# A Fourier mix and a low-rank mixer on one core: the beginning put in another order

## The chip, the cores and the metric

The kernel runs on one core of a Trainium2 chip. A core has five engines that work side by side, each through its own list of instructions in order: PE (TensorE, matrix products), DVE (VectorE), ACT (ScalarE), POOL (GpSimd) and SP (SyncE, which here only issues transfers). Transfers run on DMA engines; SP has one queue for them and POOL another. Semaphores tie the lists together. The metric is the device time of one execution in microseconds (us). Lower is better.

## The reference

The input x is 8 batches of 3136 rows by 256 columns, in float32. The first part takes a Fourier transform along the rows and one along the columns and keeps the real part. The second part is a mixer with a low-rank product over the rows (U is 3136 x 32, V is 32 x 3136) and a two-layer network over the columns:

```python
def _attn_ref(x):
    X = np.fft.fft(x, axis=1)
    X = np.fft.fft(X, axis=2)
    return X.real.astype(np.float32)

def _moe_ref(x, U, V, w_ch1, w_ch2):
    xt = x.transpose(0, 2, 1)
    h = xt @ U @ V
    u = x + h.transpose(0, 2, 1)
    ch = np.maximum(u @ w_ch1, 0.0) @ w_ch2
    return (u + ch).astype(np.float32)
```

## The kernel before

**Tables.** The transform over the rows is a matrix product with a table of sines (`tabs[0]`, called tabs in the profile) and one of cosines (`tabs[1]`, called tabc). Both are made on the chip at the start. DVE makes a phase (`phase`, L157 and L159: a multiply-add and a mask), ACT takes its sine (`sine`, L164). Four of the eight row groups are "odd" (`pho`) and are computed in full; four are "even" (`phe`), computed in half and mirrored by a copy on ACT (`mirror_even`, L238). The odd cosines are copies of odd sines, read backwards (`cosine_odd`, L243, on ACT). The even cosines take two steps on ACT (`cosine`, L170 and L171) and a mirror copy. `halve` (L226, DVE) halves one row group of a table.

**U.** U is loaded in two directions (UF by a gather on POOL, UR on SP), folded on DVE (`fold_u`, L181 to L186) and multiplied by the tables on PE (`transform_u`, L214, 32 small products at a time). For the sines this is `us`, for the cosines `uc`; each has four steps: product, copy back into the table by ACT (L219, L220), product, copy back.

**Folding x.** One batch of x at a time lies in `xf` (rows forwards, gathered by POOL: `load_f`) and `xr` (rows backwards, by SP: `load_r`), each in two halves a = 0, 1 on 98 partitions. Row 0 needs its own transfer to the 99th partition (`load_0`, by SP). DVE folds both along the columns (`along_d`, L249 and L251, into EOF_ and EOR_; POOL copies two lone columns, `alone`, L255), then folds the two directions together (`mirror`, L258, into EOS) and the two halves (`half`, L262, into G). G of batch 0 is made in two parts: columns 0 to 127 and 256, 257 first, then columns 128 to 255.

**Transform and mixer.** `seq` (L297) multiplies G by the tables on PE, 8 steps for a batch; ACT copies one product out (L301) and DVE adds and subtracts (L310 to L315). `chan` (L322, L324) is the transform over the columns with two small matrices MSN and MC, made from phases `pd`; ACT writes S and T (L326). `lowrank` (L334, L337) makes the left factor `TA`; its last line (L338, DVE) fills a row of the right factor `VA`. Then the rows of all batches are worked through in 49 chunks of 512: `front` (L360 on PE, L368 on DVE) makes u, `first_product` (L380 on PE, L382 on ACT) the hidden layer, `second_product` (L396 on PE, L402 to L405 on DVE) the output.

**Order.** The beginning, up to `front(0)`, stands in an order written by hand (`manual_schedule`). After it a scheduler orders the instructions of each engine from the order of the calls; the steps of batch b+1 are spread over the chunks of batch b by due times.

Of the kernel before, what the change touches and what calls it, by code (L numbers as in the profile page):

```python
# [27 lines left out]
def kernel(  # L28
# [42 lines left out]
    def load_0(t, dst_f, dst_r, b, w):  # L71


        lo = t.offset + b * S * w
        nc.sync.dma_start(out=dst_f[PQ:KP],
                          in_=bass.AP(t.tensor, lo + (NI - 1) * w,
                                      [[w, 1], [HALF * w, 2], [-w, NI], [1, w]]))
        nc.sync.dma_start(out=dst_r[PQ:KP].rearrange("p a i d -> p a (i d)"),
                          in_=bass.AP(t.tensor, lo, [[w, 1], [HALF * w, 2], [1, NI * w]]))

    def load_x(b):
        for a in range(2):
# [22 lines left out]
    for a in range(2):  # L105
        gather(UF[:PQ, a].rearrange("p i d -> p (i d)"), moe_U, S // 8 - 1,
               xidx[:PQ, 0, a:a + 1], 8 * R, R)
    load_0(x, xf, xr, 0, D)
    for a in range(2):
        load_r(0, a)  # L110
    for a in range(2):
        load_f(0, a)
    lrow = cpool.tile([P, 2, P], FP32, name="lrow")
    pcol = cpool.tile([P, 1], FP32, name="pcol")
    nc.gpsimd.iota(lrow[:], pattern=[[0, 2], [1, P]], base=0, channel_multiplier=0,
# [39 lines left out]
    def phase(y, a_ap, col_ap, bits):  # L155

        nc.vector.tensor_scalar(y.bitcast(FP32), a_ap, col_ap, float(2 ** (23 - bits)),  # L157
                                op0=AL.mult, op1=AL.add)
        nc.vector.tensor_single_scalar(y, y, 2 ** bits - 1, op=AL.bitwise_and)  # L159

    def sine(out_, y, bits, sgn):
        unit = TWO_PI / 2 ** bits
        pp = out_.shape[0]
        nc.scalar.activation(out_, y, AF.Sin, scale=-sgn * unit,  # L164
                             bias=(c_pi if sgn > 0 else c_npi)[:pp])
# [36 lines left out]
    def transform_u(typ):  # L202

        for pk in (1, 0):
            def contract(pk=pk):
                pu = PU[typ, pk] = psum.tile([P, NI, R], FP32, tag="dft", name="pu", bufs=3)
                for io in range(NI):
                    pn = (io + 1) % 2
                    m = kp(io)
                    j0 = NQ - 1 - (4 * 97 + (io + 1) // 2)  # L210
                    ks = ktiles(pk)
                    for n, i in enumerate(ks):
                        w = tabs[typ][:kp(i), i, pn, j0:j0 + 4 * (m - 1) + 1:4]
                        nc.tensor.matmul(pu[:m, io, :], w, GU[pn][:kp(i), typ, i, :],  # L214
                                         start=(n == 0), stop=(n == len(ks) - 1))
# [24 lines left out]

    def cosine_odd(i):

        nc.scalar.activation(cells(1, i, 1, 1, NQ - 1, 0), cells(0, i, NQ - 2, -1, NQ - 1, 1),  # L243
                             AF.Copy, scale=1.0 if i % 4 == 0 else -1.0)

    def along_d(a, src, dst, part):
        lo, hi = src[:, a, :, 1:128], src[:, a, :, 255:128:-1]
# [80 lines left out]
    def lowrank(b):  # L328
        d = ST[b]
        pt = psum.tile([R, 256], FP32, tag="dft", name="ptt", bufs=3)  # L330
        n = 0
        for typ in range(2):
            for par in range(2):
                nc.tensor.matmul(pt[:], d["tab"][:, typ, par, :], MDT[typ][:],  # L334
                                 start=(n == 0), stop=(n == 3))
                n += 1
        nc.scalar.copy(TA[b % 2][:R, :], pt[:])  # L337
        nc.vector.tensor_tensor(VA[b % 2][R:R + 1, HALF + 1:S], d["S"][0:1, HALF - 1:0:-1],  # L338
                                d["T"][0:1, HALF - 1:0:-1], op=AL.subtract)

# [74 lines left out]
    def transform(b):  # L415

        yield from fold(b)
        for par, typ in ([(0, 0), (1, 0), (0, 1), (1, 1)] if b == 0 else
                         [(0, 1), (0, 0), (1, 1), (1, 0)]):
            for pn in range(2):  # L420
                yield lambda par=par, typ=typ, pn=pn: seq(b, par, typ, pn)
        for ch in range(4):
            for h in range(2):
                yield lambda ch=ch, h=h: chan(b, ch, h)
        yield lambda: lowrank(b)

    CK = {}
    ST = {}
# [13 lines left out]
    def cosine_even(m, i):  # L442
        cosine(tabs[1][:, i, :, NH - 1:NQ], phe[:, m], 15)
        mirror_even(1, i)
# [12 lines left out]
    alone(0, xr, EOR_)  # L457
    for par in range(2):
        nc.gpsimd.memset(G[1][par][:, :, 258:GW].bitcast(I32), 0)
    for s in range(2):  # L460
        nc.gpsimd.memset(VA[s][:].bitcast(I32), 0)
        nc.gpsimd.memset(TA[s][:], 0.0)
        nc.gpsimd.memset(TA[s][R:R + 1, 0:1], 1.0)
        nc.gpsimd.memset(TA[s][R:R + 1, P:P + 1], -1.0)
    nc.gpsimd.iota(pint[:], pattern=[[0, 1]], base=D, channel_multiplier=-1)
    nc.gpsimd.memset(pint[0:1], P)
# [7 lines left out]
    nc.vector.memset(lrow[:, 1, 0:1], 128.0)  # L474
    nc.vector.tensor_single_scalar(pcol[:], pcol[:], 1.0 / D, op=AL.mult)
    pd = gen.tile([P, 2 * P], I32, name="pd", bufs=1)
    phase(pd[:], lrow.rearrange("p a l -> p (a l)"), pcol[:], 17)
    sine(MSN[:, 0:128], pd[:, 0:128], 17, -1)
    sine(MSN[:, 128:256], pd[:, 128:256], 17, 1)
    cosine(MC[:], pd[:], 17)  # L480
    msr = MSN[0:1].rearrange("p (l two) -> p l two", two=2)
    MDT = [MSN, MC]
    halve(1)
    uc[2]()
    uc[3]()
# [6 lines left out]
    for par in range(2):  # L492
        half(0, par, slice(0, 128))
        half(0, par, slice(256, 258))
    for a in range(2):
        along_d(a, xf, EOF_, 1)
        mirror(a, slice(128, 256), AL.add)
    for par in range(2):
        half(0, par, slice(128, 256))

    nc.gpsimd.dma_start(out=W1[:, 0, :], in_=moe_w_ch1[0:P, :])
    w1t = gen.tile([P, H], FP32, name="w1t", tag="w1t", bufs=1)
    gather(w1t[:], moe_w_ch1, D, pint[:], H, 0)
    for s in range(2):
        nc.gpsimd.dma_start(out=VA[s][:R, :], in_=moe_V)
    nc.gpsimd.dma_start(out=W2[:], in_=moe_w_ch2.rearrange("(j p) d -> p j d", p=P))
    nc.gpsimd.memset(msr[:, :, 0:1], 1.0)
    nc.gpsimd.memset(msr[:, :, 1:2], -1.0)
    nc.gpsimd.tensor_copy(W1[:, 1, :], w1t[:])

    gate = cpool.tile([1, 2], FP32, name="gate")
    nc.sync.dma_start(out=gate[:], in_=xf[0:1, 1, 0, 0:2])
    load_x(1)
# [57 lines left out]
```

## Time and profile before

| | |
|---|---|
| time, median of 3 runs | 504.72 us (503.43 to 505.47) |
| the profiled execution | 505.07 us, span 503.3 us |
| PE busy | 471.4 us (94%) |
| DVE, ACT, POOL busy | 311.3, 281.3, 52.7 us |
| PE's first seq product | 33.86 us after the span's start |
| PE's first product of a chunk (L380) | 51.47 us |

The span runs from the first to the last instruction; the execution's own time is a little longer. The profile names an instruction by line, engine and operation, with output and inputs (`eor<-xr` is written to eor from xr). What ended an idle time is named behind an arrow. "Busy" of PE is a modelled figure, since matrix products overlap.

### The profile page before, as it was taken

The numbers are of one execution on the slowest core, as the hardware profiler recorded it, in microseconds if no ns is written. First come the engines' busy times: TensorE is split into PE (matmuls) and PEld (weight loads), VectorE is DVE, ScalarE is ACT, GpSimd is POOL, SyncE is SP. The second block draws the span as 40 slices with busy tenths as digits, with TensorE's granted clock in tenths as the row PEclk, the third lists the DMA queues.
The fourth block names the chain that finished last, engine by engine and source line by source line (L and its number), as shares of the span: only waits on it lengthen the run. The fifth ranks groups of instructions, "written<-read, shape, count | busy, mean of one in ns | idle before, by whom it ended". The sixth has DMA issues, their size and how long they took to land.

```text
span 503.3 us, 8125 instructions
## 1 busy us (share of the span) xinstructions
PE 471.4 (94%) x3097; PEld 305.1 (61%) x3152; DVE 311.3 (62%) x693; ACT 281.3 (56%) x537; POOL 52.7 (10%) x79
## 2 busy tenths in 40 slices
PE   0659999999999999999999999999999999999997
PEld 0644556666566666666666666666666666666665
DVE  6984999999989776963574345344343344343343
ACT  6564634755466544665456544655466544755662
POOL 4722112222150200200000000000000000000000
PEclk9999999999999999999999999999999999999999
DMA  6596687889869982334223332333223332333433
GB/s 184 117 227 158 145 229 205 193 234 255 210 186 243 292 205 91 94 96 119 64 63 85 105 83 59 110 80 110 63 64 85 107 83 64 104 85 106 125 85 126
DMA packets 83475, 67.13 MB, mean 133 GB/s; under 512 B 53470, under 2 KB 79908, under 8 KB 80284
## 3 DMA queue, kind: packets, MB, share of 16 engines
q1 hardware_dynamic: 79868, 51.86, 39.8%
q0 software_dynamic: 3568, 14.76, 11.3%
q8 instruction: 24, 0.39, 0.3%
q14 instruction: 15, 0.12, 0.1%
HBM read 29.26 MB, written 25.69 MB: 109 GB/s over the span
## 4 chain that ended last, share of the span: by engine, by line
PE 89%; DVE 4%; ACT 3%; DMA 1%; issue 1%; POOL 0%; DVEq 0%; POOLq 0%; ACTq 0%
PE p L396 34%; PE p L380 31%; PE pt L297 14%; PE ph L360 4%; PE pst L322 2%; PE pst L324 2%; DMA uf<-in_moe_U_dram,xidx 1%; PE ptt L334 1%; PE pu L214 1%; DVE phe L157 1%; ACT tabc L171 1%; DVE eor L251 0%; DVE eof L251 0%; DVE eor L249 0%; DVE eof L249 0%
## 5 line engine op out<-in xcount | busy, mean ns | idle before, releaser
L382 ACT ACTIVATE h<-p 128x512 bf16<-128x512 f32 x392 | 218.2, 597 | 147.6 <-PE p L380 137.6
L396 PE MATMUL p<-w,h 128*128 128x256 bf16 x1568 | 203.7, 273 | 1.7 <-DVE o L405 0.8
L380 PE MATMUL p<-u,w 128*128 128x512 bf16 x735 | 201.7, 379 | 3.3 <-DVE u L368 1.2
L396 PEld LDWEIGHTS <-h 128*128 128x128 bf16 x1568 | 153.1, 98 | 60.1 <-DVE o L405 1.4
L380 PEld LDWEIGHTS <-w 128*128 128x128 bf16 x784 | 75.8, 98 | 64.1 <-issue 3.5
L402 DVE TENSOR_TENSOR o<-p,ut 128x4 f32<-128x4 f32 (+1 forms) x100 | 16.5, 165 | 137.6 <-PE p L396 136.5
L297 PE MATMUL pt<-tabc,g 98*128 98x425 bf16 (+1 forms) x256 | 57.1, 349 | 0.0
L297 PEld LDWEIGHTS <-g 98*128 98x128 bf16 (+1 forms) x384 | 38.1, 99 | 31.0 <-issue 3.0
L405 DVE TENSOR_TENSOR o<-p,ut 128x254 f32<-128x254 f32 (+1 forms) x100 | 40.9, 409 | 0.0
L404 DVE TENSOR_TENSOR o<-p,ut 128x254 f32<-128x254 f32 (+1 forms) x100 | 40.9, 409 | 0.0
L301 ACT COPY ev<-pt 128x425 f32<-128x425 f32 x32 | 16.5, 515 | 38.4 <-PE pt L297 29.8
L368 DVE TENSOR_TENSOR u<-ph,S 128x512 bf16<-128x512 f32 (+15 forms) x64 | 35.1, 558 | 0.9 <-PE ph L360 0.9
L368 DVE TENSOR_TENSOR u<-ph,T 128x512 bf16<-128x512 f32 (+15 forms) x64 | 35.0, 557 | 0.0
L297 PE MATMUL pt<-tabs,g 98*128 98x425 bf16 (+1 forms) x128 | 29.8, 357 | 0.0
L360 PE MATMUL ph<-va,ta 128*128 128x512 bf16 (+14 forms) x122 | 28.0, 327 | 0.8 <-ACT ta L337 0.5
L52 POOL DMA_INDIRECT xf<-in_x_dram,xidx x16 | 21.2, 1328 | 52.3 <-DVE eof L251 17.1
L310 DVE TENSOR_TENSOR B<-pt,ev 128x393 bf16<-128x393 f32 (+1 forms) x16 | 9.4, 585 | 23.9 <-PE pt L297 23.9
L322 PE MATMUL pst<-A,mc 128*128 128x392 bf16 (+1 forms) x64 | 21.2, 331 | 0.7 <-DVE A L310 0.7
L214 PE MATMUL pu<-gu,tabs 98*98 98x32 bf16 (+1 forms) x64 | 6.2, 252 | 16.5 <-DVE gu L185 13.0
L258 DVE TENSOR_TENSOR eos<-eof,eor 99x1024 bf16<-99x1024 bf16 (+2 forms) x34 | 21.3, 663 | 0.2
L324 PE MATMUL pst<-B,msn 128*128 128x392 bf16 (+1 forms) x64 | 21.1, 330 | 0.0
L255 POOL CAST eof<-xf 99x16 bf16<-99x16 f32 x16 | 12.3, 776 | 82.9 <-DVE eos L258 53.6
(86 smaller groups left out, 288.7 us busy)
## 6 DMA issues: line engine op xcount, KB each, us to landing
out_dram<-o SPq DMA_DIRECT2D x48, 512.0 KB
xr<-in_x_dram SPq DMA_DIRECT2D x16, 784.0 KB
ut<-u SPq DMA_TRANSPOSE x49
w<-in_moe_w_ch_dram POOLq DMA_DIRECT2D x1, 512.0 KB, 15.4
out_dram<-o SPq DMA_DIRECT2D x4, 128.0 KB
va<-in_moe_V_dram POOLq DMA_DIRECT2D x2, 196.0 KB, 13.5
xf<-in_x_dram,xidx POOLq DMA_INDIRECT x16, 7.7
w<-in_moe_w_ch_dram POOLq DMA_DIRECT2D x1, 256.0 KB, 7.5
```

Of the source, the lines that this page charges most:

```text
L52: nc.gpsimd.indirect_dma_start(out_, None, bass.AP(t.tensor, t.offset, [[w, rows], [1, w]]), bass.IndirectOffsetOnAxis(idx, 0), element_of ...
L258: nc.vector.tensor_tensor(EOS[:, a, :, cols], EOF_[:, a, :, cols], EOR_[:, a, ::-1][:, :, cols], op=op)
L297: nc.tensor.matmul(pt[:], g[:kp(i), i, col:col + P], tabs[t][:kp(i), i, par, :], start=(n == 0), stop=(n == len(mm) - 1))
L322: nc.tensor.matmul(pt[:, :hi - lo], MC[:, h * P:(h + 1) * P], d["A"][:, lo:hi], start=True, stop=False)
L324: nc.tensor.matmul(pt[:, :hi - lo], MSN[:, h * P:(h + 1) * P], d["B"][:, lo:hi], start=False, stop=True)
L360: nc.tensor.matmul(ph[:, col:col + hi - lo], TA[b % 2][:, s * P:(s + 1) * P], VA[b % 2][:, lo:hi], start=True, stop=True)
L368: nc.vector.tensor_tensor(u[:, s, col:col + hi - lo], ph[:, col:col + hi - lo], src, op=AL.add)
L380: nc.tensor.matmul(p1[:], W1[:, s, j * P:(j + 1) * P], k["u"][:, s, :], start=(s == 0), stop=(s == 1))
L382: nc.scalar.activation(k["h"][:, j, :], p1[:], AF.Relu)
L396: nc.tensor.matmul(p2[:, t % w, :], h[:, j, rs], W2[:, j, :], start=(j == 0), stop=(j == JT - 1))
L404: nc.vector.tensor_tensor(o[:, ts, 1:P], p2[:, :w, 1:P], ut[:, ts, 1:P], op=AL.add)
L405: nc.vector.tensor_tensor(o[:, ts, P + 1:D], p2[:, :w, P + 1:D], ut[:, tT, P - 1:0:-1], op=AL.add)
```

## The change

Nothing is added to or taken from the computation; the order of the beginning changes, one kind of copy moves to another engine, and two steps are cut in two.

- DVE makes all eight phases and ACT all eight sine masks first; U's fold follows.
- `cosine_odd` is done by GpSimd (a multiply by 1 or -1) in place of ACT. In GpSimd's list it stands behind the first `alone`.
- GpSimd's zeros (`VA`, `TA`, the tail of G of odd batches) and the index `pint` move behind the first fold of batch 0. A small copy out of G (`gate`) stands ahead of the zeros.
- `us` comes ahead of `uc` throughout.
- The phases and matrices over the columns (`pd`, MSN, MC) move behind the first part of G.
- V's transfers move from one place to two, each behind its zeros; `load_f(1)` moves ahead of the second of them. SP's small gate transfer waits for `w1t` in place of `xf`; then `load_r(1)` and `load_0(1)` follow.
- `load_0` sends the backward row in two transfers, one for each half, written as 16 pieces, and for batch 0 it stands behind `load_r`.
- The last line of `lowrank` becomes a step of its own, `difference`. For batch 0 it comes behind `front(0)`, for the others it is one more step of the spread (26 in place of 25).

```diff
-        nc.sync.dma_start(out=dst_r[PQ:KP].rearrange("p a i d -> p a (i d)"),
-                          in_=bass.AP(t.tensor, lo, [[w, 1], [HALF * w, 2], [1, NI * w]]))
+        for a in range(2):
+            nc.sync.dma_start(
+                out=dst_r[PQ:KP, a].rearrange("p i d -> p (i d)").rearrange("p (e f) -> p e f", e=16),
+                in_=bass.AP(t.tensor, lo + a * HALF * w,
+                            [[w, 1], [NI * w // 16, 16], [1, NI * w // 16]]))
...
-    load_0(x, xf, xr, 0, D)
     for a in range(2):
         load_r(0, a)
     for a in range(2):
         load_f(0, a)
+    load_0(x, xf, xr, 0, D)
...
-        nc.scalar.activation(cells(1, i, 1, 1, NQ - 1, 0), cells(0, i, NQ - 2, -1, NQ - 1, 1),
-                             AF.Copy, scale=1.0 if i % 4 == 0 else -1.0)
+        nc.gpsimd.tensor_single_scalar(cells(1, i, 1, 1, NQ - 1, 0),
+                                       cells(0, i, NQ - 2, -1, NQ - 1, 1),
+                                       1.0 if i % 4 == 0 else -1.0, op=AL.mult)
...
+    def difference(b):
+        d = ST[b]
         nc.vector.tensor_tensor(VA[b % 2][R:R + 1, HALF + 1:S], d["S"][0:1, HALF - 1:0:-1],
                                 d["T"][0:1, HALF - 1:0:-1], op=AL.subtract)
...
-    fold_u()
-    for i in range(0, NI, 2):
-        cosine_odd(i)
-    us, uc = list(transform_u(0)), list(transform_u(1))
-    us[0]()
-    uc[0]()
...
     for m, i in enumerate((7, 5, 3, 1)):
         phase(phe[:, m], krow[:KP, :, NH - 1:], ncol[:KP, i:i + 1], 15)
         sine(tabs[0][:, i, :, NH - 1:NQ], phe[:, m], 15, 1)
         mirror_even(0, i)
-    us[1]()
-    cosine_even(0, 7)
-    uc[1]()
-    cosine_even(1, 5)
-    cosine_even(2, 3)
+    fold_u()
+    halve(0)
     for part in range(2):
         along_d(0, xr, EOR_, part)
     alone(0, xr, EOR_)
-    for par in range(2):
-        nc.gpsimd.memset(G[1][par][:, :, 258:GW].bitcast(I32), 0)
-    for s in range(2):
-        nc.gpsimd.memset(VA[s][:].bitcast(I32), 0)
-        nc.gpsimd.memset(TA[s][:], 0.0)
...
-    halve(0)
+    for i in range(0, NI, 2):
+        cosine_odd(i)
+    us, uc = list(transform_u(0)), list(transform_u(1))
+    us[0]()
+    cosine_even(0, 7)
+    cosine_even(1, 5)
+    us[1]()
     us[2]()
+    cosine_even(2, 3)
     us[3]()
+    uc[0]()
     cosine_even(3, 1)
+    uc[1]()
     for part in range(2):
         along_d(1, xr, EOR_, part)
     alone(1, xr, EOR_)
+    halve(1)
+    uc[2]()
+    uc[3]()
...
+    gate = cpool.tile([P, 4], FP32, name="gate")
+    nc.gpsimd.tensor_copy(gate[0:1, 2:3], G[0][1][0:1, 0, 128:129])
+    for s in range(2):
+        nc.gpsimd.memset(VA[s][:].bitcast(I32), 0)
+        nc.gpsimd.dma_start(out=VA[s][:R, :], in_=moe_V)
+        nc.gpsimd.memset(TA[s][:], 0.0)
...
+        if s == 0:
+            nc.gpsimd.tensor_copy(W1[:, 1, :], w1t[:])
+            nc.gpsimd.dma_start(out=W2[:], in_=moe_w_ch2.rearrange("(j p) d -> p j d", p=P))
+            load_f(1, 0)
+            load_f(1, 1)
+    for par in range(2):
+        nc.gpsimd.memset(G[1][par][:, :, 258:GW].bitcast(I32), 0)
+    nc.sync.dma_start(out=gate[0:1, 0:2], in_=w1t[0:1, 0:2])
...
-    for step in list(transform(0))[8:]:
+    for step in list(transform(0))[8:-1]:
         step()
     setup.close()
     cp = ctx.enter_context(tc.tile_pool(name="cp", bufs=2))
     front(0)
+    difference(0)
```

More of the change, by code (lines that the diff above doesn't have):

```diff
@@ L425, in transform @@
         yield lambda: lowrank(b)
+        yield lambda: difference(b)
     CK = {}
@@ L434 @@
         sine(tabs[0][:, i, :, :NQ], pho[:, m], 15, 1)
-    fold_u()
-    for i in range(0, NI, 2):
-        cosine_odd(i)
-    us, uc = list(transform_u(0)), list(transform_u(1))
-    us[0]()
-    uc[0]()
-    def cosine_even(m, i):
-        cosine(tabs[1][:, i, :, NH - 1:NQ], phe[:, m], 15)
-        mirror_even(1, i)
     for m, i in enumerate((7, 5, 3, 1)):
@@ L457, with cosine_even @@
     alone(0, xr, EOR_)
-    for par in range(2):
-        nc.gpsimd.memset(G[1][par][:, :, 258:GW].bitcast(I32), 0)
-    for s in range(2):
-        nc.gpsimd.memset(VA[s][:].bitcast(I32), 0)
-        nc.gpsimd.memset(TA[s][:], 0.0)
[L463 to L466, printed above, removed]
-    halve(0)
+    for i in range(0, NI, 2):
+        cosine_odd(i)
+    def cosine_even(m, i):
+        cosine(tabs[1][:, i, :, NH - 1:NQ], phe[:, m], 15)
+        mirror_even(1, i)
+    us, uc = list(transform_u(0)), list(transform_u(1))
[3 more added lines that the diff above has]
+    us[1]()
     us[2]()
+    cosine_even(2, 3)
     us[3]()
+    uc[0]()
     cosine_even(3, 1)
+    uc[1]()
     for part in range(2):
@@ L473 @@
     alone(1, xr, EOR_)
[L474 to L482, printed above, removed]
     halve(1)
@@ L494 @@
         half(0, par, slice(256, 258))
+    nc.vector.memset(lrow[:, 1, 0:1], 128.0)
+    nc.vector.tensor_single_scalar(pcol[:], pcol[:], 1.0 / D, op=AL.mult)
+    pd = gen.tile([P, 2 * P], I32, name="pd", bufs=1)
+    phase(pd[:], lrow.rearrange("p a l -> p (a l)"), pcol[:], 17)
+    sine(MSN[:, 0:128], pd[:, 0:128], 17, -1)
+    sine(MSN[:, 128:256], pd[:, 128:256], 17, 1)
+    cosine(MC[:], pd[:], 17)
+    msr = MSN[0:1].rearrange("p (l two) -> p l two", two=2)
+    MDT = [MSN, MC]
     for a in range(2):
@@ L499 @@
         half(0, par, slice(128, 256))
+    nc.gpsimd.iota(pint[:], pattern=[[0, 1]], base=D, channel_multiplier=-1)
+    nc.gpsimd.memset(pint[0:1], P)
     nc.gpsimd.dma_start(out=W1[:, 0, :], in_=moe_w_ch1[0:P, :])
@@ L503 @@
     gather(w1t[:], moe_w_ch1, D, pint[:], H, 0)
-    for s in range(2):
-        nc.gpsimd.dma_start(out=VA[s][:R, :], in_=moe_V)
-    nc.gpsimd.dma_start(out=W2[:], in_=moe_w_ch2.rearrange("(j p) d -> p j d", p=P))
     nc.gpsimd.memset(msr[:, :, 0:1], 1.0)
     nc.gpsimd.memset(msr[:, :, 1:2], -1.0)
[L509 to L513, printed above, removed]
-    for step in list(transform(0))[8:]:
+    gate = cpool.tile([P, 4], FP32, name="gate")
[4 more added lines that the diff above has]
+        nc.gpsimd.memset(TA[s][:], 0.0)
+        nc.gpsimd.memset(TA[s][R:R + 1, 0:1], 1.0)
+        nc.gpsimd.memset(TA[s][R:R + 1, P:P + 1], -1.0)
+        if s == 0:
[6 more added lines that the diff above has]
+    nc.sync.dma_start(out=gate[0:1, 0:2], in_=w1t[0:1, 0:2])
+    for a in range(2):
+        load_r(1, a)
+    load_0(x, xf, xr, 1, D)
+    for step in list(transform(0))[8:-1]:
         step()
```

## The prediction

> **What bounds the kernel now.** I read the busy time by stages first, then the chain of work that ended last, then the timelines of DVE, ACT and POOL over the first 65 us. Stages (start:end and length, then busy us of PE, its weight loads, DVE, ACT, POOL, then clock, DMA share, GB/s):
>
> ```profile
> 0.00:34.00 34.00, 12.31 (x129) 12.22 (x130) 29.50 (x60) 21.92 (x39) 17.97 (x36) 1.00 0.71 174
> 34.00:64.22 30.22, 26.91 (x137) 13.77 (x136) 21.51 (x35) 14.55 (x31) 7.02 (x9) 1.00 0.71 161
> 64.22:200.00 135.78, 134.61 (x870) 85.50 (x887) 121.68 (x230) 73.83 (x141) 25.00 (x31) 1.00 0.84 214
> 200.00:350.00 150.00, 148.98 (x977) 96.55 (x995) 77.63 (x189) 87.33 (x168) 2.72 (x4) 1.00 0.33 90
> ```
>
> From 64.22 us on PE idles 1.2 us in 136 and 1.0 in 150, and the change leaves its products as they are. So time can only move before 64.22, by when PE's unbroken work begins. The chain there (start, us, what):
>
> ```profile
> 3.66 6.86 DMA uf<-in_moe_U_dram,xidx
> ...
> 13.24 2.82 DVE phe L157
> 16.08 1.96 DVE phe L159
> 18.07 0.63 ACT tabs L164
> ...
> 30.30 0.54 ACT tabc L238
> 30.84 0.04 issue
> 30.89 3.13 PE pu L214 x32
> 34.02 11.20 PE pt L297 x48
> ```
>
> U's landing holds the even phases, they hold ACT, ACT's tables hold PE's last U product, and that the first seq product. The two phases of 2.8 and 2.0 us are not work: the next ones take 0.41 and 0.37. The timelines show what lies beside them (start, us):
>
> ```profile
> 13.16 2.89 DVE L157 TENSOR_SCALAR phe<-krow,ncol 99x394 f32<-99x394 f32 x1
> 16.08 1.95 DVE L159 TENSOR_SCALAR phe<-phe 99x394 int32<-99x394 int32 x1
> 17.95 0.41 DVE L157 TENSOR_SCALAR phe<-krow,ncol 99x394 f32<-99x394 f32 x1
> ```
>
> ```profile
> 13.25 0.98 POOL L459 MEMSET g<- 99x504 int32 x2
> 14.18 1.40 POOL L461 MEMSET va<- 128x1568 int32 x1
> ...
> 20.49 0.98 POOL L255 CAST eor<-xr 99x16 bf16<-99x16 f32 x1 [1.95 <-DMA xr<-in_x_dram]
> ...
> 37.03 1.04 POOL L509 CAST w<-w1t 128x1024 bf16<-128x1024 f32 x1 [5.17 <-DMA w1t<-in_moe_w_ch_dram,pint]
> 44.59 0.25 POOL L255 CAST eof<-xf 99x16 bf16<-99x16 f32 x1 [4.03 <-DMA xf<-in_x_dram,xidx]
> ```
>
> DVE's phases stand while POOL's zeros run one after another. The other way round, POOL's lone-column copy, 0.25 us alone, took 0.98 while a fold ran on DVE.
>
> **The change, part by part.**
>
> *Even phases and masks.* DVE is done with the odd phases at 7.60; four even pairs of 0.75 end at 10.6. ACT is done with the odd sines at 8.6, then four sine and mirror pairs of 1.09 (18.07 to 22.49 before) end at 13.0. The old chain (fold, 4.0 us of stalls, late masks) is gone. Two even cosines of 1.75 end at 16.4. What is late next: ACT's copy-back of `us[1]`. In the changed program it waits for the fourth of POOL's cosine copies, which read the same table, and the other two cosines stand behind it in ACT's list.
>
> *When the copies start.* They stand behind POOL's first `alone`, which needs x's row 0, and that transfer is moved behind `load_r`. Before, `alone` ran at 12.87. Of the landings of the second backward half the trace has twelve between 12.1 and 16.0 and two at 20.3 and 20.4: the two DMA engines that also carried row 0. Bounds for the new landing are thus 12.9 and 20.4. With row 0 behind, the two should run like the twelve, all issued 0.7 us sooner (1.3 us of row-0 issues gone from ahead of them, 2.72 to 4.01, and one U row of 0.6 added); then 0.7 us for the forward row (16 pieces on two engines, 38.85 to 39.55 for batch 1) and one large row of 0.5 between. I take 16.5. U may land some 0.5 to 1 us later, as large rows now start sooner; its products have cover until the copies end.
>
> *How long the copies take.* No row shows GpSimd multiplying. Nearest is its cast of 1024 elements in 1.04 us: 784 elements give 0.80. The lower end is that; the upper is twice the 1.04, 2.1, for a reversed two-byte read and an arithmetic step. I take 0.9, by the cast, so 3.6 us for four. ACT loses 4 x 0.77 = 3.1 us that lay in an idle stretch (6.5 us before 18.07): no gain on the path. The Trainium skill's GPSIMD Engine Reference (Elementwise — side-by-side cycle accounting) puts a tight loop at 1.8 cycles an element; at its 1.2 GHz that is an estimate of 1.2 us a copy, and the sum below would be 1.2 us longer.
>
> *Folds beside copies.* At 16.5 DVE starts its two folds of the first half, 1.125 each, from the same landing as POOL. By the 20.49 row a POOL reader waits for the fold that runs; by the 13.16 row DVE then waits until POOL's run of operations ends. I take two folds first: copies from 18.8 to 22.4. Bounds: no wait at all (copies 16.8 to 20.4) and all four folds first (copies end at 24.7).
>
> *From the copies to PE.* ACT: copy-back 0.42, cosine 1.75, copy-back 0.41, cosine 1.84 (all from the chain) = 4.4: 26.8. PE's last U product 3.0 (30.89 to 33.86): 29.9. DVE: two folds 2.25, halve 0.35, first part of G 5.36 (26.16 to 31.52 before), of which its first half-tile comes 0.75 sooner: 22.4 + 7.2 = 29.6. The first seq product starts at about 29.9 in place of 33.86: a gain of 4.0 us.
>
> *Column matrices.* Phases, 0.8 us, stand ahead of G's second part (5.0): it is ready near 36.2, needed 7.5 us after the first product (33.86 to 41.34), at 37.4. MSN and MC are needed at 42. Cost 0; cover 1.2 us, beyond which each microsecond counts.
>
> *POOL's list behind the gate.* The gate copy waits for G's second part (36.2); behind it stand zeros 1.4, V's issue 0.6, TA's zeros 0.7, W1's cast 1.0 (40.0, needed at 29.9 + 17.6 = 47.5), W2's issue 0.9, then the gathers of batch 1. V, issued at 38, has until 46. W2's data took 2.5 us behind V's before: in by 46, needed at 52.8. The gathers took 3.2 us each: 48.9 and 52.1. SP's gate now waits for `w1t` (issued near 24, landing by 32 where it is less crowded than before); the backward loads then have until 51. DVE wants the first gather at 48.9. Cover nil: 0 taken, up to 2 us lost.
>
> *Chunk 1.* In the changed order DVE has, behind u of chunk 0: `difference` 0.9, four folds of batch 1 (4.5) and only then u of chunk 1 (1.3). Before, two folds stood there. PE has 16 products until it needs it, 3.8 us (52.01 to 55.77), so it stands 2.9 us. Work from there to its wait for o (55.77 to 63.40, 7.6 us) now ends at 14.3 us after u, with o ready at 13.3; before, PE went on at 64.22, 12.2 us after u. Loss 2.1, less 0.2 as L338 no longer stands ahead of u, and something regained in the smaller waits behind: 1.7.
>
> *Later batches.* One more SP issue of 0.6 per batch and `difference` as a step: SP and DVE have room behind PE's 99%. Cost 0; without that cover a wait like the 0.82 us before 64.22 for each of seven batches, so -0.5 to +2.
>
> Sum: -4.0 + 1.7 = -2.3 us on the profiled 505.07, so 502.8. The median is 0.35 below the profiled execution: 502.4, and I give 502.5.
>
> **The rivals.**
>
> A, this sum: own range 500.8 to 504.8 (landing 15.5 to 17.5, copies 0.8 to 1.1).
>
> B, copies and folds do not hinder each other: copies end at 20.4, PE starts at 27.9 by ACT's path (DVE's G by 26.6). -6.0 + 1.7 = -4.3: 500.4. For it: the fold beside the 0.98 us copy was not longer than others (1.22 against 1.21). Against: that copy was tiny.
>
> C, slower by the port: strict turns, one copy, one fold, or all four folds first. Copies end 2.3 us later: 504.8, no gain. The Trainium skill's SBUF — State Buffer (two separate sides) says that a DVE operation with two SBUF inputs and a GpSimd one that reads SBUF lock each other out for a whole instruction. The 0.98 us row agrees with that.
>
> D, slower by the copy: GpSimd takes 1.7 to 2.1 us for each. Place: ACT behind `us[1]`. Each 0.1 us costs 0.4; above 0.9 + 2.3/4 = 1.5 us a copy the change loses. At 2.0: +4.4 - 2.3, so 506.8. For it: nothing in this trace shows the operation. Against: zeros, casts and index rows of POOL all run near 0.8 to 1.0 ns an element.
>
> E, slower by the row: row 0's small pieces take turns with the large gathered rows and land at 20.4, +3.9: 506.3. For: the two late engines took 1.0 to 1.2 us for each large row, in turns with the other queue. Against: forward rows came in one stretch for batch 1.
>
> **How the numbers follow.** Chances: A 45%, B 20%, C 12%, D 12%, E 11%. The time is A's. The range leaves out the fast half of B and the slow half of D and E: 499.8 to 506.8. Half a per cent, 2.5 us, is about what a measurement can tell from no change: faster is below 502.2, slower above 507.2. Faster: B and under half of A, 0.40. Slower: the ends of D and E, 0.11. Within: 0.49.
>
> **What would show it.** Right: no zeros beside the phases, phases of 0.4 us; ACT's copy-back of tabs idle some 5 us on POOL's tabc copies; four copies near 0.9 us; first seq product near 30; PE idle about 3 us for u of chunk 1; PE near 99% from 65 on. Wrong: the first `alone` after 18.5 (E), copies over 1.5 us (D), a fold over 1.3 us or not (A against B), DVE waiting for the gather of batch 1, or PE idle over 1% past 70 us.

## The result and the profile after

The changed kernel is slower: 511.31 us (median of 4 runs, 510.82 to 512.11) against 505.10 for the kernel before in the same session, a ratio of 1.0129 (95% interval 1.0100 to 1.0159). The forecast was 502.5, the range 499.8 to 506.8. The profiled execution took 511.09 us with a span of 509.3, 6.0 us longer than before.

Stages of the changed kernel, cut at its own events (start:end and length, then busy us of PE, its weight loads, DVE, ACT, POOL, then clock, DMA share, GB/s):

```profile
0.00:37.10 37.10, 12.63 (x129) 12.27 (x130) 27.89 (x60) 17.48 (x31) 19.98 (x25) 1.00 0.44 120
37.10:54.76 17.66, 15.39 (x71) 7.36 (x72) 7.50 (x18) 7.66 (x19) 10.68 (x21) 1.00 0.94 218
54.76:71.00 16.24, 13.38 (x67) 7.17 (x68) 16.20 (x22) 8.60 (x16) 5.56 (x5) 0.89 0.80 190
71.00:200.00 129.00, 128.20 (x834) 81.88 (x848) 116.01 (x217) 71.31 (x136) 21.82 (x29) 1.00 0.85 220
```

The cuts are the first seq product (37.10, before 33.86), the first product of a chunk (54.76, before 51.47) and 71, by when PE's unbroken work runs again. The first stage is 3.24 us longer, the transform as long as before (17.66 against 17.61). From 54.76 to the end it takes 454.5 us, before 451.8 (503.3 less 51.47). I call this last length the tail: it is 2.7 us longer. From 71 on PE idles 0.8 us in 129, so nothing is lost there. The whole loss of 6.0 lies ahead of 71: 3.3 at the beginning, 2.7 in the tail.

The beginning, in the chain that ended last of the changed kernel (start, us, what):

```profile
4.29 13.70 DMA xr<-in_x_dram
18.11 0.20 POOL eor L259
...
19.34 10.29 POOL tabc L246 x4
...
33.54 0.54 ACT tabc L241
34.13 3.13 PE pu L217 x32
```

x's row 0 is awaited until 18.1, then GpSimd's four copies take 10.3 us, then come ACT's 4.4 and PE's 3.0. The copies are the longest piece that an engine works on. The timelines of the changed kernel show the same by engine (start us, us, engine, line, operation, then idle before and what ended it):

```profile
8.38 0.42 DVE L160 TENSOR_SCALAR phe<-krow,ncol 99x394 f32<-99x394 f32 x1
8.83 0.37 DVE L162 TENSOR_SCALAR phe<-phe 99x394 int32<-99x394 int32 x1
...
20.35 1.84 DVE L253 TENSOR_TENSOR eor<-xr 99x1016 bf16<-99x1016 f32 x1
...
19.34 10.28 POOL L246 TENSOR_SCALAR tabc<-tabs 99x784 bf16<-99x784 bf16 x4
...
29.65 0.34 ACT L222 CAST tabs<-pu 98x224 bf16<-98x224 f32 x1 [13.26 <-POOL tabc L246]
...
22.53 0.27 PE L217 MATMUL pu<-gu,tabc 98*98 98x32 bf16 x1 [3.29 <-POOL tabc L246]
25.40 0.27 PE L217 MATMUL pu<-gu,tabc 98*98 98x32 bf16 x1 [2.60 <-POOL tabc L246]
27.54 0.28 PE L217 MATMUL pu<-gu,tabc 98*98 98x32 bf16 x1 [1.86 <-POOL tabc L246]
29.68 2.85 PE L217 MATMUL pu<-gu,tabc 98*98 98x32 bf16 x29 [1.86 <-POOL tabc L246]
```

The phase stall is gone: phase 0.42, mask 0.37. But ACT stood 13.26 us until the copies were done. PE's U product took them one by one as they came, so its four waits mark their ends: 22.5, 25.4, 27.5, 29.7. The first two ran beside DVE's folds of float32 rows (3.1 and 2.9 us); the third ran beside one fold of EOS (1.30 us, two-byte numbers) and the fourth beside nothing, and both took 2.14.

The tail, in windows of 2 us of the changed kernel (same columns as the stages):

```profile
60.00:62.00 2.00, 0.39 (x1) 0.11 (x2) 2.00 (x3) 0.03 (x1) 1.76 (x1) 1.00 0.17 25
62.00:64.00 2.00, 1.81 (x8) 0.97 (x8) 2.00 (x4) 1.19 (x2) 0.00 (x0) 0.63 0.66 242
64.00:66.00 2.00, 2.00 (x8) 1.04 (x7) 2.00 (x3) 0.07 (x1) 0.00 (x0) 0.51 1.17 291
```

PE stands 2.38 us for u of chunk 1 while DVE is full. Then the granted clock is about 0.5 until 66, and 1.00 behind that. In that time 8 products of L404 take 1.91 us and 4 of L388 1.58; a little later the same take 1.04 and 1.03, so with the first three of L388 (1.14 against 0.81) the lower clock costs about 1.75 us. Stand and clock make 4.1; the 0.82 and 0.31 us that PE stood there before no longer appear, which leaves 3.0 of the measured 2.7.

### The profile page after: what moved, and what is told of

It reads as the page before. It is cut to its first block, busy times and chain, and to the rows that moved or that the text cites. A ratio compares the mean times of both kernels' runs of the same rounds, so it can differ in the third digit from the quotient of the medians.

```text
span 509.3 us, 8153 instructions
## 1 busy us (share of the span) xinstructions
PE 473.2 (93%) x3097; PEld 306.3 (60%) x3152; DVE 309.7 (61%) x693; ACT 279.7 (55%) x533; POOL 59.7 (12%) x84
## 4 chain that ended last, share of the span: by engine, by line
PE 89%; DMA 3%; POOL 2%; issue 2%; DVE 2%; ACT 1%; SPq 1%; DVEq 0%; POOLq 0%
PE p L404 35%; PE p L388 31%; PE pt L301 14%; PE ph L368 4%; DMA xr<-in_x_dram 3%; POOL tabc L246 2%; PE pst L326 2%; PE pst L328 2%; PE ptt L338 1%; PE pu L217 1%; DVE u L376 0%; SPq L75 0%; ACT tabc L174 0%; DVE eof L253 0%; DVE eor L255 0%
## 5 line engine op out<-in xcount | busy, mean ns | idle before, releaser
L388 PE MATMUL p<-u,w 128*128 128x512 bf16 x731 | 202.4, 380 | 4.9 <-DVE u L376 3.7
L404 PE MATMUL p<-w,h 128*128 128x256 bf16 x1568 | 203.7, 273 | 1.7
L404 PEld LDWEIGHTS <-h 128*128 128x128 bf16 x1568 | 153.6, 98 | 59.9 <-issue 0.7
L388 PEld LDWEIGHTS <-w 128*128 128x128 bf16 x784 | 76.0, 98 | 65.1 <-issue 4.2
L301 PEld LDWEIGHTS <-g 98*128 98x128 bf16 (+1 forms) x384 | 38.1, 99 | 32.9 <-issue 3.2
L305 ACT COPY ev<-pt 128x425 f32<-128x425 f32 x32 | 16.5, 515 | 32.9 <-PE pt L301 22.2
L314 DVE TENSOR_TENSOR B<-pt,ev 128x393 bf16<-128x393 f32 (+1 forms) x16 | 9.4, 586 | 27.7 <-PE pt L301 27.5
L52 POOL DMA_INDIRECT xf<-in_x_dram,xidx x16 | 18.8, 1175 | 56.0 <-DVE o L413 22.1
L253 DVE TENSOR_TENSOR eor<-xr 99x1016 bf16<-99x1016 f32 x16 | 20.0, 1251 | 5.7 <-DMA xr<-in_x_dram 5.7
L330 ACT CAST S<-pst 128x392 bf16<-128x392 f32 (+1 forms) x32 | 15.7, 492 | 8.9 <-PE pst L328 8.9
```

The source lines that it names most:

```text
L253: nc.vector.tensor_tensor(dst[:, a, :, 1:128], lo, hi, op=AL.subtract)
L301: nc.tensor.matmul(pt[:], g[:kp(i), i, col:col + P], tabs[t][:kp(i), i, par, :], start=(n == 0), stop=(n == len(mm) - 1))
L388: nc.tensor.matmul(p1[:], W1[:, s, j * P:(j + 1) * P], k["u"][:, s, :], start=(s == 0), stop=(s == 1))
L404: nc.tensor.matmul(p2[:, t % w, :], h[:, j, rs], W2[:, j, :], start=(j == 0), stop=(j == JT - 1))
```

## The experiments

Theory 1: GpSimd is slow at the copies, and they hold ACT and so the first seq product. Theory 2: the late row 0 is the loss. Theory 3: the loss behind the beginning is the order of DVE's work around chunk 1. The rivals of each stand in the expectations. All results, with the first seq product, the first product of a chunk and the tail of the profiled execution (us):

| label | seq | chunk | tail | median | ratio to before (95%) |
|---|---|---|---|---|---|
| before | 33.86 | 51.47 | 451.8 | 504.1 to 505.1 by session | |
| after | 37.10 | 54.76 | 454.5 | 511.31 | 1.0129 (1.0100 to 1.0159) |
| act_copies | 27.96 | 46.40 | 455.6 | 503.97 | 1.0006 (0.9980 to 1.0031) |
| copies_first | 29.45 | 46.72 | 457.1 | 504.16 | 1.0001 (0.9978 to 1.0023) |
| price (one run) | 28.36 | 46.68 | 456.1 | 504.60 | |
| row0_early | 28.91 | 46.66 | 454.5 | 503.87 | 0.9996 (0.9972 to 1.0019) |
| two_copies | 33.30 | 51.68 | 454.5 | 507.98 | 1.0088 (1.0060 to 1.0115) |
| u1_first | 37.74 | 56.29 | 459.8 | 515.01 | 1.0207 (1.0151 to 1.0263) |
| u1_two | 37.30 | 54.27 | 453.4 | 510.35 | 1.0131 (1.0086 to 1.0176) |
| diff_alone | 32.30 | 50.17 | 452.6 | 504.49 | 1.0013 (0.9987 to 1.0039) |
| zeros_late | 29.50 | 47.86 | 451.8 | 501.34 | 0.9936 (0.9913 to 0.9959) |
| late_dve | 29.77 | 47.70 | 451.9 | 501.64 | 0.9949 (0.9928 to 0.9969) |
| best | 25.54 | 43.56 | 455.2 | 501.78 | 0.9951 (0.9928 to 0.9975) |
| early_x | 27.79 | 55.24 | 453.0 | 507.10 | 1.0071 (1.0042 to 1.0100) |

Read the columns with care. The tails repeat: 451.8, 451.8 and 451.9 in before, zeros_late and late_dve, and 454.5 in after, row0_early and two_copies. The starts do not: diff_alone has the beginning of before, yet its seq product came at 32.30, because the first even phase took 0.93 there in place of 2.89. The stretch from the first seq product to the first chunk product does not either. In the same code it took 17.66 us in after, 16.97 in u1_two and 18.55 in u1_first. The first seq products start 0.35 us apart and the later ones 0.18, and it was 14, 10 and 18 products that went at the slower pace. So differences under some 1.6 us between single profiles say little unless they lie in the tail.

**The copies on ACT again (act_copies).**

```diff
-        nc.gpsimd.tensor_single_scalar(cells(1, i, 1, 1, NQ - 1, 0),
-                                       cells(0, i, NQ - 2, -1, NQ - 1, 1),
-                                       1.0 if i % 4 == 0 else -1.0, op=AL.mult)
+        nc.scalar.activation(cells(1, i, 1, 1, NQ - 1, 0), cells(0, i, NQ - 2, -1, NQ - 1, 1),
+                             AF.Copy, scale=1.0 if i % 4 == 0 else -1.0)
```

> Only the engine of the odd cosines is put back: ACT copies them, everything else as in the changed kernel. Theory 1 (GpSimd's copies set the beginning): ACT makes its four copies by 16.2 in its idle stretch, ends its last copy-back near 24.1, PE's last U product ends near 27.1; DVE's folds from 18.07 run unhindered (1.22 each) and the first part of G is ready near 28.1. First seq product near 28.2 in place of 37.1, time near 502.4. Rival (the start is held by something else: row 0's landing at 18.0 or DVE's own work): the first seq product stays later than 33 and the time above 507.

Two lines of PE's timeline in this run:

```profile
27.96 1.60 PE L301 MATMUL pt<-tabs,g 98*128 98x425 bf16 x4 [1.08 <-DVE g L266]
...
54.30 0.39 PE L388 MATMUL p<-u,w 128*128 128x512 bf16 x1 [3.44 <-DVE u L376]
```

The first seq product came at 27.96 as expected, 9.1 us sooner, now held by DVE's G. So, with all else as changed, the copies' engine alone takes the loss at the beginning away; row0_early below shows that this is not the only way. The time is 503.97, level with the kernel before, not 502.4: the tail grew by 1.1 us, because batch 1's x was not there yet (DVE waited 1.07 us for it) and PE stood 3.44 us for u of chunk 1.

**The copies ahead of the first lone-column copy (copies_first).**

```diff
-    alone(0, xr, EOR_)
     for i in range(0, NI, 2):
         cosine_odd(i)
+    alone(0, xr, EOR_)
```

> The copies stay on GpSimd but stand ahead of its first lone-column copy, so that they start when the odd sines are there (8.6) and run beside DVE's phases and U's fold, not beside the folds of x. Theory 1a (GpSimd is slow at this operation by itself): about 2.1 us each, copies end at 17 to 19. Theory 1b (the folds of x stretched them, alone they are as fast as its cast): about 0.9 us each, copies end near 12.5. Either way DVE's path then holds PE: first seq product near 28.2, time near 502.4; if U's fold and the phases are stretched by the copies, up to 2 us more.

Timelines of DVE and POOL in this run:

```profile
7.50 1.49 DVE L160 TENSOR_SCALAR phe<-krow,ncol 99x394 f32<-99x394 f32 x1
9.03 1.31 DVE L162 TENSOR_SCALAR phe<-phe 99x394 int32<-99x394 int32 x1
...
7.93 8.91 POOL L246 TENSOR_SCALAR tabc<-tabs 99x784 bf16<-99x784 bf16 x4
```

Far from the folds of x the four still took 8.91 us, 2.2 each: 1a, not 1b. They stretched DVE in turn: phase 1.49 in place of 0.42, mask 1.31 in place of 0.37, so that PE's first U product came at 17.71 in place of 13.25. DVE lost nothing by it, since it reached x's first fold at 18.25, when x had just landed. PE's U products ended later, so the first seq product came at 29.45, 1.5 us behind that of act_copies. The time is that of act_copies.

**The price of the operation by itself (price).** The copies of the table are on ACT, as above. Three further operations write to a spare tile:

```diff
+    nc.gpsimd.tensor_copy(scr[0:1, 3, 0, 0:1], tabs[0][0:1, 7, 0, 1:2])
+    nc.gpsimd.tensor_single_scalar(scr[:, 0, :, 1:NQ], cells(0, 0, NQ - 2, -1, NQ - 1, 1), -1.0, op=AL.mult)
+    nc.gpsimd.tensor_single_scalar(scr[:, 1, :, 1:NQ], cells(0, 2, 1, 1, NQ - 1, 0), -1.0, op=AL.mult)
+    nc.gpsimd.tensor_copy(scr[:, 2, :, 1:NQ], cells(0, 4, NQ - 2, -1, NQ - 1, 1))
```

> The changed kernel with the odd cosines on ACT, and three more operations on GpSimd into a spare tile, from 14 to 18.4 us, where DVE waits for x and runs nothing: the odd cosine's multiply with its read backwards, the same multiply reading forwards, and a plain copy reading backwards, 784 elements each. Theory 1 (the operation is slow by itself): the first takes 2.0 to 2.3 us with DVE idle. If the backward read is what costs, the second takes about 0.9 and the third about 2.1; if the multiply is what costs, the second about 2.1 and the third about 0.8. Rival (only DVE beside it stretched it): all three 0.8 to 1.1 us.

Timelines of POOL and DVE in this run (L452 multiplies and reads backwards, L453 multiplies and reads forwards, L454 copies and reads backwards):

```profile
14.21 2.19 POOL L452 TENSOR_SCALAR scr<-tabs 99x784 bf16<-99x784 bf16 x1
16.39 2.16 POOL L453 TENSOR_SCALAR scr<-tabs 99x784 bf16<-99x784 bf16 x1
18.50 1.52 POOL L454 COPY scr<-tabs 99x784 bf16<-99x784 bf16 x1
...
18.11 1.22 DVE L253 TENSOR_TENSOR eor<-xr 99x1016 bf16<-99x1016 f32 x1 [4.13 <-DMA xr<-in_x_dram]
19.24 1.85 DVE L255 TENSOR_TENSOR eor<-xr 99x1016 bf16<-99x1016 f32 x1
```

With DVE idle one copy of the table's kind (a multiply, read backwards) takes 2.19 us, and reading forwards changes nothing. The plain copy took 1.52 beside two folds, one of which took 1.85 in place of 1.22. So the operation is slow by itself, and its direction is not the cause; the multiply costs at least 0.6 more than the copy. This is one run.

**Row 0 first again (row0_early).**

```diff
+    load_0(x, xf, xr, 0, D)
     for a in range(2):
         load_r(0, a)
     for a in range(2):
         load_f(0, a)
-    load_0(x, xf, xr, 0, D)
```

> Only batch 0's row 0 is loaded ahead of the backward halves again, as in the kernel before. Theory 2 (the late landing is a part of the loss by itself): the first lone-column copy runs near 13 in place of 18.1, the four copies end 4 to 6 us sooner, near 24, first seq product 31 to 33, time 505 to 507. Rival (the large rows of x land late whatever row 0 does): lone-column copy still after 17, time 510 to 512. By theory 1 the four copies still take 8.4 us or more here.

POOL's timeline in this run:

```profile
11.14 0.25 POOL L259 CAST eor<-xr 99x16 bf16<-99x16 f32 x1 [3.04 <-DMA xr<-in_x_dram]
11.33 10.11 POOL L246 TENSOR_SCALAR tabc<-tabs 99x784 bf16<-99x784 bf16 x4
```

The lone-column copy ran at 11.14 in place of 18.11; the four copies took as long as before, 10.11, but ended 8.2 us sooner. The first seq product came at 28.91 (31 to 33 expected), and the time, 503.87, is below the 505 to 507 expected. So theories 1 and 2 are not rivals: the loss needs a slow copy and a late start, and any one of three edits (act_copies, copies_first, this) brings the time from 1.3% above the kernel before to level with it.

**Two of the four copies (two_copies).**

```diff
+        if i < 4:
+            nc.gpsimd.tensor_single_scalar(cells(1, i, 1, 1, NQ - 1, 0),
+                                           cells(0, i, NQ - 2, -1, NQ - 1, 1),
+                                           1.0 if i % 4 == 0 else -1.0, op=AL.mult)
+            return
+        nc.scalar.activation(cells(1, i, 1, 1, NQ - 1, 0), cells(0, i, NQ - 2, -1, NQ - 1, 1),
+                             AF.Copy, scale=1.0 if i % 4 == 0 else -1.0)
```

> The changed kernel with two of the four odd cosines on GpSimd, the other two on ACT in its idle stretch. By the copies' measured length (the four ended at 22.5, 25.4, 27.5 and 29.7 by PE's waits) ACT's wait ends at 25.4 in place of 29.65, the first seq product comes at 32.9 in place of 37.1, 1.0 before that of the kernel before. Behind it the changed order costs 2.7 us (span less first product of a chunk: 454.5 against 451.8). Time 506 to 507.5: slower than before with an earlier start. Rival (with two copies less the folds of x collide less and the start falls under 31): time 503 to 505.

The two took 6.01 us, the seq product came at 33.30 (32.9 expected), and the time, 507.98, is 0.5 above the 506 to 507.5 expected. The tail is 454.5, as after. The beginning is then no later than before (first chunk product 51.68 against 51.47), and the kernel still loses 0.9%: what remains, 2.7 us in the tails, is the changed order around chunk 1.

**u of chunk 1 at once (u1_first), and behind two folds (u1_two).** The first edit:

```diff
-    front(0)
+    front(0); front(1)
     difference(0)
...
-            if j == 3 and c + 1 < NCH:
+            if j == 3 and 0 < c < NCH - 1:
```

> The changed kernel with u of chunk 1 made right behind u of chunk 0, ahead of the difference and the folds of batch 1; the beginning stays as it is (first seq product at 37.1). Theory 3 (the loss behind the beginning is PE's stand for u of chunk 1 and the lower clock after it): PE does not stand over 0.5 us between 56 and 62, the granted clock stays at 1.00 from 62 to 66 where it was 0.50, time 507 to 508.5. Rival (the loss comes from later batches, 26 steps in place of 25, or PE only stands later for its outputs): time within 1 us of 511.3.

The second:

```diff
-            if j == 3 and c + 1 < NCH:
+            if j == (0 if c == 0 else 3) and c + 1 < NCH:
```

> The changed kernel with two folds of batch 1 ahead of u of chunk 1, as before, in place of four; the difference stays ahead of them, the beginning as it is (first seq product 37.1). Theory 3a (the bunch of folds ahead of one u is the loss): PE stands 0.5 to 1.0 us for u of chunk 1 in place of 2.4 and 0.8 to 1.8 for the outputs or u of chunk 2, the granted clock stays at 1.00; time 508 to 509.5. Theory 3b (DVE has too much work from 54 to 75, whatever its order): PE's stand moves to chunk 2 and is as long, over 2 us, with the clock at 0.50 after it; time 510.5 to 513.

PE's timeline in u1_first:

```profile
71.75 1.89 PE L388 MATMUL p<-u,w 128*128 128x512 bf16 x4 [3.93 <-DVE u L376]
```

And in u1_two:

```profile
68.14 0.72 PE L404 MATMUL p<-w,h 128*128 128x256 bf16 x5 [1.38 <-DVE o L413]
...
69.95 0.60 PE L388 MATMUL p<-u,w 128*128 128x512 bf16 x2 [1.09 <-DVE u L376]
```

With u of chunk 1 at once, its stand was gone and the clock stayed at 1.00 up to 71, but eight folds then stood ahead of u of chunk 2: PE stood 3.93 us there, and the kernel is 0.8% slower than the changed one. My theory 3 as first put fell: the stand moved. With two folds ahead of u of chunk 1 and six ahead of the first outputs, PE's stands are 1.4 and 1.1 us, the clock stays at 1.00 and the tail of the profiled execution is 453.4, 1.1 shorter. The median, 510.35, lies between what 3a and 3b gave, and by the ratios (1.0131 and 1.0129) no gain can be told. By the tails, which are of one profile each, the order of the folds accounts for 1.1 of the 2.7 us and the difference behind u of chunk 0 for 0.8 (the next run). The other 0.8 is not settled by any run.

**The difference as its own step, alone (diff_alone).** To the kernel before:

```diff
+    def difference(b):
+
+        d = ST[b]
...
+        yield lambda: difference(b)
...
-    for step in list(transform(0))[8:]:
+    for step in list(transform(0))[8:-1]:
...
     front(0)
+    difference(0)
```

> The kernel before with one part alone: the difference is a step of its own, behind u of chunk 0 for batch 0 and one of 26 steps for the others. On DVE it then stands ahead of the two folds and of u of chunk 1. Theory (every us that DVE does between u of chunk 0 and the folds of batch 1 is paid): folds start 0.9 us later after u of chunk 0, PE stands about 0.7 us for u of chunk 1 and about 1.7 in place of 0.8 for the outputs; time 0.5 to 1.5 us above the kernel before. Rival (26 steps disturb the later batches): PE idles over 1 us past 100 us, time 2 us or more above.

The tail is 452.6, 0.8 longer than before, with PE's stand for the outputs at 1.4 in place of 0.8 us and a new one of 0.2 for u of chunk 1; the time (ratio 1.0013) can't be told from before. The seq product at 32.30 is no effect of this edit, which leaves the beginning as it is. 26 steps in place of 25 cost nothing that shows: past 70 us PE had no wait.

**The zeros alone (zeros_late).** To the kernel before; W1's issue and `pint` stay ahead of them:

```diff
-    for par in range(2):
-        nc.gpsimd.memset(G[1][par][:, :, 258:GW].bitcast(I32), 0)
-    for s in range(2):
-        nc.gpsimd.memset(VA[s][:].bitcast(I32), 0)
...
     gather(w1t[:], moe_w_ch1, D, pint[:], H, 0)
+    gz = cpool.tile([1, 2], FP32, name="gz")
+    nc.gpsimd.tensor_copy(gz[0:1, 0:1], G[0][1][0:1, 0, 0:1])
+    for par in range(2):
+        nc.gpsimd.memset(G[1][par][:, :, 258:GW].bitcast(I32), 0)
+    for s in range(2):
+        nc.gpsimd.memset(VA[s][:].bitcast(I32), 0)
...
```

> The kernel before with one part of the change alone: GpSimd's zeros wait for the first part of G. Theory (the phase stall held the beginning): the first even phase and mask take 0.4 us each in place of 2.89 and 1.95, ACT's even masks and PE's last U product come 4.0 us sooner, first seq product near 29.9 in place of 33.86, if DVE's G (31.5 before, 4 us sooner too) is ready. The time follows only as far as DVE has room for batch 1's folds: by the runs with an early start so far (starts of 28 to 29, times no lower than before) 0 to 2 us less, 502 to 504; if the whole gain were kept, 500. Rival (something else holds the masks): start at 33 or later, time 504 to 505.

DVE and PE in this run:

```profile
12.85 0.41 DVE L157 TENSOR_SCALAR phe<-krow,ncol 99x394 f32<-99x394 f32 x1
13.30 0.37 DVE L159 TENSOR_SCALAR phe<-phe 99x394 int32<-99x394 int32 x1
...
29.50 1.58 PE L297 MATMUL pt<-tabs,g 98*128 98x425 bf16 x4
```

The phases take 0.41 and 0.37, the seq product comes at 29.50, 4.36 sooner than in the profile of before (2.80 sooner than in diff_alone, where the stall was shorter), the tail is that of before (451.8), and the time is 501.34, 3.6 us below the kernel before in that session (504.93). With one part of the change and none of the rest it beats both kernels, and no other run has a lower median.

**Two edits for the beginning and one for chunk 1 (best).** To the changed kernel: row 0 first (as in row0_early), two folds ahead of u of chunk 1 (as in u1_two), and the copies on DVE:

```diff
-        nc.gpsimd.tensor_single_scalar(cells(1, i, 1, 1, NQ - 1, 0),
+        nc.vector.tensor_single_scalar(cells(1, i, 1, 1, NQ - 1, 0),
...
     halve(0)
+    for i in range(0, NI, 2):
+        cosine_odd(i)
     for part in range(2):
         along_d(0, xr, EOR_, part)
     alone(0, xr, EOR_)
-    for i in range(0, NI, 2):
-        cosine_odd(i)
```

> The changed kernel with three edits: the odd cosines copied by DVE right behind U's fold (0.42 us each, by the halving of 786 elements), row 0 of batch 0 loaded first again, and two folds ahead of u of chunk 1. DVE folds the first backward half from 16, the second from 18.2, G's first part is ready near 26.0; ACT never waits for the copies, PE's last U product ends near 24. First seq product 26.0, first product of a chunk 43.7 in place of 51.47. Behind it 0.5 to 2 us more than in the kernel before: time 498 to 500. Rival (DVE's folds of batch 1 hold PE whatever the start): PE stands over 2 us between 47 and 56, clock 0.50 after it, time 501 to 504.

DVE in this run:

```profile
13.50 1.17 DVE L246 TENSOR_SCALAR tabc<-tabs 99x784 bf16<-99x784 bf16 x4
...
46.63 1.22 DVE L253 TENSOR_TENSOR eof<-xf 99x1016 bf16<-99x1016 f32 x1 [1.53 <-DMA xf<-in_x_dram,xidx]
```

The seq product came at 25.54, 8.3 us sooner than before, and the four copies took DVE 1.17 us together. But the time, 501.78, is no better than zeros_late: the tail is 3.4 longer. DVE waited 1.53 us for batch 1's x and PE stood 1.50, 1.41 and 1.09 us in place of 0.82 and 0.31. The 498 to 500 expected was missed. The time lies in the rival's range, but the rival's signs, a stand over 2 us and a clock of 0.50, do not show.

**Batch 1's x earlier (early_x).** To best: V's zeros and issue ahead of the gathers, the gathers ahead of W1's cast and W2, SP's gate on xf in place of w1t, two folds ahead of u of chunk 0:

```diff
-    nc.gpsimd.tensor_copy(gate[0:1, 2:3], G[0][1][0:1, 0, 128:129])
...
-            nc.gpsimd.tensor_copy(W1[:, 1, :], w1t[:])
-            nc.gpsimd.dma_start(out=W2[:], in_=moe_w_ch2.rearrange("(j p) d -> p j d", p=P))
             load_f(1, 0)
             load_f(1, 1)
+            nc.gpsimd.tensor_copy(W1[:, 1, :], w1t[:])
+            nc.gpsimd.dma_start(out=W2[:], in_=moe_w_ch2.rearrange("(j p) d -> p j d", p=P))
...
-    nc.sync.dma_start(out=gate[0:1, 0:2], in_=w1t[0:1, 0:2])
+    nc.sync.dma_start(out=gate[0:1, 0:2], in_=xf[0:1, 1, 0, 0:2])
...
+    steps = list(transform(1)); steps[0]()
     front(0)
```

> The best kernel so far by its start (DVE copies, row 0 first, two folds ahead of u of chunk 1), with batch 1's x fetched earlier: V's and TA's zeros of even batches stand ahead of GpSimd's wait, the forward gathers directly behind it, W1's cast and W2 behind those; SP's gate waits for batch 0's last forward rows, as in the kernel before; two folds of batch 1 stand ahead of u of chunk 0 on DVE. Theory (the end is set by when DVE can begin batch 1's folds: span less that moment was 451.4 before, 452.2 in the run named best): x lands near 39 to 40 in place of 46.6, two folds are made in DVE's 4.3 us of idle time ahead of u of chunk 0, no wait for the gather; PE stands under 1 us for u of chunk 1; span 494 to 496, time 496.5 to 499. Rival (the landings crowd each other, x lands no sooner than 43 and holds u of chunk 0, or V comes late): time 501 or more.

DVE in this run:

```profile
52.23 1.22 DVE L253 TENSOR_TENSOR eof<-xf 99x1016 bf16<-99x1016 f32 x1 [11.94 <-DMA xf<-in_x_dram]
```

And SP in this run:

```profile
41.38 0.64 SPq L524 DMA_DIRECT2D gate<-xf  x1
...
43.83 0.63 SPq L75 DMA_DIRECT2D xf<-in_x_dram  x1
```

The time is in the rival's range, but the cause is another one, and it lies in the edit. The gathers did come earlier: the first was issued at 30.7 and landed at 37.4 (37.3 and 46.6 in best), and the second had landed by 41.4 (50.6 in best). But SP's gate reads xf and stands behind these gathers, which write to xf. So it waited for batch 1's own rows, until 41.4; the expectation has it wait for batch 0's. Row 0 of batch 1 stands behind the gate on SP: it was issued at 43.83 in place of 30.10 and landed at 52. DVE's two folds waited 11.94 us for it, with u of chunk 0 behind them, and PE stood 10.89 us. So what an earlier x is worth was not tested. The profiled execution is a long one of this kernel (510.0 against a median of 507.1).

**Zeros late, copies on DVE (late_dve).** To zeros_late: `cosine_odd` on DVE behind the even phases, and `uc[0]` behind it.

> The kernel before with two edits: zeros behind the first part of G (as in the run named zeros_late) and the odd cosines copied by DVE behind the even phases, in 1.2 us for four. ACT's 3.1 us of copies are gone, so PE's last U product ends near 26.4; DVE's first part of G, 27.05 in zeros_late, comes 1.2 later, near 28.3. First seq product 28.3 in place of 29.5; x of batch 1 lands at 46.6 as in both faster runs and does not hold DVE. Span 498.0 to 499.0, time 499.5 to 501. Rival (start and x's landing both no sooner): as zeros_late, 501.3.

The seq product came at 29.77, not 28.3, and the time is 501.64, as zeros_late. The rival held: ACT's copies had lain in its idle time ahead of the even phases (it idled 5.39 us there in this run), so taking them away moved nothing. ACT's work still began when U had landed and DVE had made the even phases.

## Why the prediction was wrong

By its own steps:

- *Even phases and masks*: right. Phases 0.42 and 0.37, two even cosines done at 16.4. zeros_late shows what the stall alone was worth: 4.36 us at the first seq product against the profile of before (0.3 of it because U landed sooner), and 3.6 us in the medians.
- *When the copies start*: off by 0.5, by two errors that nearly cancelled. The row landed 1.6 us late, at 18.1 in place of 16.5, but the copies waited for one fold of DVE and not for two, so they started at 19.34 in place of 18.8.
- *How long the copies take*: here the prediction failed. 0.9 us each was taken, by GpSimd's cast of 1024 elements in 1.04, with 2.1 as the upper end. One copy takes 2.19 us alone, above the upper end, and the four took 10.28 in place of 3.6: 6.7 us. The sentence from the Trainium skill's GPSIMD Engine Reference (Elementwise — side-by-side cycle accounting) gave an estimate of 1.2 us for a copy; the run that prices it shows 2.19, nearly twice that, and the measurement decides.
- *Folds beside copies*: the size was small, but the turns were another. DVE did not wait until the copies were done: it went on with its folds beside them. The first two copies lost 1.7 us together to DVE's folds, and one fold took 1.84 in place of 1.22. DVE also waited 3.30 us for a lone-column copy that stood behind the copies on POOL; this was not foreseen, and ACT's path was longer anyway.
- *From the copies to PE*: right, 4.43 and 2.97 us for 4.4 and 3.0.
- *Column matrices* and *POOL's list behind the gate*: right at 0 in the changed kernel. With an earlier start (act_copies, copies_first, best) the wait for batch 1's x that the step named did come, 1.1 to 1.7 us.
- *Chunk 1*: the stand for u of chunk 1 was foreseen, the size of the loss off by 1.0: 2.7 in place of 1.7. PE stood 2.38 us, less than the 2.9 taken, but the granted clock fell to 0.5 behind it, about 1.75 us that no step held.
- *Later batches*: right at 0.

The repaired sum: 502.5 plus 7.2 for the end of the copies (29.6 in place of 22.4) plus 1.0 for the tail is 510.7; 511.3 was measured. Rival D named mechanism, place and break-even point (1.5 us a copy), and was given 12%: its 506.8 was worked out at 2.0 us a copy, without the collisions. Rival E was a part of it, though its own sign did not show (the first `alone` ran at 18.11, and the sign was after 18.5): the late row put the copies on the path, and in row0_early, with it early, copies just as slow cost nothing.

## What to carry to other kernels

When the trace has no row for the operation that an engine takes over, work out first at which price the change turns, and give more chance to the wrong side of it the further the nearest row is in operation and type. Then ask whether the new work stands behind a wait that it does not need: here GpSimd was idle for 10 us ahead of the copies, and moving one line (copies_first) took 7.65 us off the start. A gain at a beginning is kept only as far as what comes next is ready sooner too. zeros_late lost nothing in the tail; of its 4.36 us, 0.75 went between the seq product and the first chunk product, where 18 products in place of 14 went at the slower pace. best, 4 us earlier still, kept none of that. Batch 1's x landed at 46.6 in both, and that this is the reason is argued, not shown, since early_x did not test it.

## What the runs showed of the hardware

- GpSimd took 2.19 us to multiply 99 x 784 two-byte elements by a constant, ACT 0.84 for the same copy in two_copies, and DVE 1.17 for four of them in best.
- A GpSimd operation of this kind slows DVE's short operations beside it: phase 0.42 to 1.49 and mask 0.37 to 1.31 in copies_first, a fold 1.22 to 1.84 in after. The zeros did the same to a phase (2.89) and a mask (1.95) in the kernel before, but beside the folds of zeros_late, where they ran from 28.2 to 32.8, the folds kept their 1.21.
- The granted clock fell to 0.5 for some 3 us or more after PE had stood about 2.4 us or longer (after, row0_early, two_copies, act_copies, copies_first, u1_first, early_x), and stayed at 1.00 after stands of 1.4 to 1.5 us (u1_two, best). The Trainium skill's TensorE: Matmul & The Clock Gate (Part 1: The HAM clock gate) puts the idle window that lowers the clock at about 3.4 us; the trace shows the fall after a stand of 2.38 us, or 3.0 us with one product in it. In early_x it fell at 46.1, under 2 us after the last product that the trace shows. The measurement decides.
- The first 10 to 18 seq products start 0.35 us apart and the later ones 0.18, though the granted clock reads 1.00 all along. The number differs between runs with the same beginning (10 in u1_two, 14 in after, 18 in u1_first); why stays open.
